# An MLP kernel's opening: the first transpose of x for one tile in place of two, and the loads behind it in another order

## The chip, the cores and the metric

The kernel runs on one core of a Trainium2 chip. The metric is the device time of one execution in microseconds, as the median of several runs. Times inside an execution come from a profile of one execution and count from its first instruction.

## The reference

The computation is a two-layer feed-forward block on 2048 tokens, in bf16. x has 640 features, the hidden layer 1728.

```
x: (1, 2048, 640)   w1: (640, 1728)   w2: (1728, 640)
h   = einsum("bsd,df->bsf", x, w1)
h   = silu(h)
out = einsum("bsf,fd->bsd", h, w2)
```

## The kernel before

TensorE contracts over the 128 partitions, so x must stand in SBUF with its features on partitions. `xT` holds x in this form: 5 tiles of 128 features (index k) by 2048 tokens. The form is made by DMA transposes straight from DRAM, all issued from the SP queue. The tokens are cut into 4 chunks of 512. w1 stands in `w1s` as 5 slabs, one for each k, of 1728 columns. The columns of h form 13 blocks of 128 (index ft) and a tail of 64.

The unit of work in the first stage is `step`: for one k, one block ft and one chunk, two matmuls of 64 columns of w1 each against 512 tokens, into the two halves of one PSUM bank. Five steps (k = 0 to 4) complete a block of one chunk; ScalarE then applies silu and writes `hT`.

The first chunk is treated apart, because its data have yet to arrive. Its first 8 blocks (1024 columns of w1) occupy the 8 PSUM banks at once, and the work goes k by k: for each k a sweep over the 8 blocks, so 8 steps need only tile k of x and the first 1024 columns of slab k. `opening` (line 197) first runs dummy matmuls on a zeroed tile `z` (line 132: 13 of 128 columns and one pair of 64 columns, each against 256 columns), then waits for the first transpose and the first 5 blocks of slab 0, does the sweep of k = 0, and calls `sweep` (line 192) for k = 1, 2, 3. Each sweep begins with a wait for its slab and its tile. The sweep for k = 4 follows, with the silus; then blocks 8 to 12 of chunk 0, five steps each, and then chunks 1 to 3, each behind a wait for its five transposes. TensorE works in program order, so a wait holds all that stands behind it.

The order of the transfers is written out by hand. `early` puts instructions ahead of the program's start-up barrier on an engine. The ACT queue issues the first 5 blocks of slab 0 (160 KB). The SP queue issues, in this order (lines 123 and 148 to 157): the transpose of tiles 0 and 1 for chunk 0; the other 3 blocks of slab 0 (96 KB); slab 1 (256 KB, 8 blocks); slab 2; the transpose of tile 2; slab 3; the transpose of tiles 3 and 4; slab 4; two loads with the remaining columns of all slabs (320 KB and 560 KB). Then come 15 transposes, one for each tile of chunks 1 to 3 (line 163), and the four loads of w2. Each transfer has a semaphore of its own; the five transposes of a chunk share one. `turned` (line 90) issues a transpose, `slab` (line 118) a part of a slab.

The second stage multiplies hT by w2, which has long arrived, evacuates the results through VectorE and ScalarE, and stores them. The change does not touch it.

Of the kernel before, what the change touches and what calls it, by code (L numbers as in the profile page):

```python
# [9 lines left out]
def bass_standalone__dense_activation_silu__prompt_kernel(  # L10
# [13 lines left out]
    P = 128  # L24
# [5 lines left out]
    SCH = 512  # L30
# [8 lines left out]
    pe, act, dve, pool, sp = nc.tensor, nc.scalar, nc.vector, nc.gpsimd, nc.sync  # L39

    with ExitStack() as es:
# [18 lines left out]
        def sem(name):  # L60
            s = es.enter_context(nc.semaphore(name))
            count[s.name if hasattr(s, "name") else name] = 0
            return [s, 0]

        def tick(ins, s, n=1):
            ins.then_inc(s[0], n)
            s[1] += n
            return (s, s[1])

        def wait(eng, *points):  # L70
            for pt in points:
                if pt is None:
                    continue
                s, v = pt
                key = (id(eng), id(s))
                if seen.get(key, 0) < v:
                    eng.wait_ge(s[0], v)
                    seen[key] = v
# [6 lines left out]
        def load(eng, out_ap, in_ap):  # L85
            s = sem(f"s_ld{n_dma[0]}")
            n_dma[0] += 1
            return tick(eng.dma_start(out=out_ap, in_=in_ap), s, 16)

        def turned(c0, c1, k0, k1):  # L90
            s = sem(f"s_tr{n_dma[0]}")
            n_dma[0] += 1
            return tick(sp.dma_start_transpose(
                out=xT[:, k0:k1, c0:c1], in_=xf[c0:c1, k0 * P:k1 * P]), s, 16)

        ET = mybir.EngineType

        def early(emit, engine, arrived=True):
            n = len(nc.main_func.blocks[0].instructions)
            r = emit()  # L100
            lst = nc.main_func.blocks[0].instructions
            new = lst[n:]
            del lst[n:]
            at = next(
                i for i, ins in enumerate(lst)
                if ins.opcode == ("EventSemaphore" if arrived else "Drain") and ins.engine == engine
            )
            lst[at:at] = new
            return r
# [4 lines left out]
        NO = NB  # L114
# [3 lines left out]
        def slab(eng, k, f0=0, f1=NO):  # L118
            return load(eng, w1s[:, k, f0 * P:f1 * P], w1_v[:, k, f0 * P:f1 * P])

        ld_w1 = {}
        ld_t = {}
        ld_t[0] = ld_t[1] = early(lambda: turned(0, SCH, 0, 2), ET.SP, False)
        ld_w1[0] = early(lambda: slab(act, 0, 0, NA), ET.Activation, False)
        p_z = early(lambda: tick(dve.memset(z[:, :], 0.0), s_dve), ET.DVE, False)  # L125

# [2 lines left out]
        def dummies(n, w):  # L129
            for _ in range(n):  # L130
                for c0 in range(0, P, w):
                    pe.matmul(ps[c0:c0 + w, 3, 0:HB], lhsT=z[:, 0:w], rhs=z[:, :],  # L132
                              start=True, stop=True)

        def first_dummies():
            wait(pe, p_z)
            dummies(13, P)
            dummies(1, HC)

        p_warm = early(lambda: tick(pool.memset(warm[:, :], 0.0), s_pool), ET.Pool, False)  # L140
# [5 lines left out]
        early(warm_up, ET.Activation, False)  # L146

        ld_w1b = early(lambda: slab(sp, 0, NA, NO), ET.SP, False)
        ld_w1[1] = early(lambda: slab(sp, 1), ET.SP, False)
        ld_w1[2] = early(lambda: slab(sp, 2), ET.SP, False)  # L150
        ld_t[2] = early(lambda: turned(0, SCH, 2, 3), ET.SP, False)
        ld_w1[3] = early(lambda: slab(sp, 3), ET.SP, False)
        ld_t[3] = ld_t[4] = early(lambda: turned(0, SCH, 3, DT), ET.SP, False)
        ld_w1[4] = early(lambda: slab(sp, 4), ET.SP, False)
# [28 lines left out]
        def step(b, k, ft, c0, c1, start=False, stop=False):  # L183
            for h0 in (0, HC):
                ins = mm(ps[h0:h0 + HC, b, :], w1s[:, k, ft * P + h0:ft * P + h0 + HC],
                         xT[:, k, c0:c1], start, stop, shared=True)
            return ins

        def part(k, ft, c0, c1, start=False, stop=False):
            return step(ft, k, ft, c0, c1, start, stop)  # L190

        def sweep(k, c0, c1, *waits):
            wait(pe, *waits)
            for ft in range(NO):
                part(k, ft, c0, c1)

        def opening():
            first_dummies()
            wait(pe, ld_t[0], ld_w1[0])
            for ft in range(NO):  # L200
                if ft == NA:
                    wait(pe, ld_w1b)
                part(0, ft, 0, SCH, start=True)
            for k in range(1, DT - 1):
                sweep(k, 0, SCH, ld_w1[k], ld_t[k])
# [206 lines left out]
```

## Time and profile before

| | us |
|---|---|
| median of 3 runs (lowest, highest) | 124.34 (124.25, 124.39) |
| the profiled execution | 124.57 |
| its span, first to last instruction | 123.1 |
| TensorE busy | 120.7 (98%) |
| ScalarE busy | 38.8 (32%) |
| VectorE busy | 6.9 (6%) |

The chain that ended last is TensorE for 98% of the span. Nothing but TensorE's own pace stands on it after its first instruction at 0.39 us, apart from pieces of 0.3 us and less. How the opening's transfers were issued from SP, and how long each took from its issue to its landing:

| transfer | issued at | issue took | landed after |
|---|---|---|---|
| transpose of tiles 0 and 1 | 0.00 | 1.33 | 3.4 |
| slab 0, last 3 blocks | 1.39 | 0.56 | 3.1 |
| slab 1 | 2.00 | 0.42 | 3.3 |
| slab 2 | 2.46 | 0.43 | 3.5 |
| transpose of tile 2 | 2.94 | 1.16 | 3.6 |
| slab 3 | 4.14 | 0.58 | 3.3 |
| transpose of tiles 3 and 4 | 4.76 | 1.24 | 3.7 |
| slab 4 | 6.04 | 0.59 | 4.1 |
| remaining columns, first load | 6.67 | 0.44 | 4.4 |
| remaining columns, second load | 7.15 | 0.53 | 5.6 |
| first transpose of chunk 1 | 8.07 | 1.46 | 5.2 |
| fifth transpose of chunk 1 | 13.48 | 2.21 | 4.4 |

The ACT queue's 160 KB of slab 0 were issued at 0.12 and landed after 2.4. A landing is issue time plus the last column. In the lines of the profile, PE stands for TensorE's matmuls, PEld for its weight loads, SPq and ACTq for the queues of SP and ScalarE, ACT for ScalarE, DVE for VectorE and POOL for GpSimd.

### The profile page before, as it was taken

The numbers are of one execution on the slowest core, as the hardware profiler recorded it, in microseconds if no ns is written. First come the engines' busy times: TensorE is split into PE (matmuls) and PEld (weight loads), VectorE is DVE, ScalarE is ACT, GpSimd is POOL, SyncE is SP. The second block draws the span as 40 slices with busy tenths as digits, with TensorE's granted clock in tenths as the row PEclk, the third lists the DMA queues.
The fourth block names the chain that finished last, engine by engine and source line by source line (L and its number), as shares of the span: only waits on it lengthen the run. The fifth ranks groups of instructions, "written<-read, shape, count | busy, mean of one in ns | idle before, by whom it ended". The sixth has DMA issues, their size and how long they took to land.

```text
span 123.1 us, 2300 instructions
## 1 busy us (share of the span) xinstructions
PE 120.7 (98%) x1056; PEld 59.5 (48%) x1057; DVE 6.9 (6%) x11; ACT 38.8 (32%) x67; POOL 0.3 (0%) x5
## 2 busy tenths in 40 slices
PE   8999999999999999999999999999999999999993
PEld 5455555555555555555544444444444444444452
DVE  0000000000000000000000022002201300222001
ACT  4002975555555555555530011001101200110110
POOL 0000000000000000000000000000000000000000
PEclk9999999999999999999999999999999999999999
DMA  6999935555992000000000004202200220023112
GB/s 146 263 248 315 135 86 108 104 87 92 280 392 77 0 0 0 8 0 0 0 0 5 0 12 113 51 0 107 107 0 5 107 107 0 5 107 117 53 67 83
DMA packets 19625, 10.42 MB, mean 85 GB/s; under 512 B 13728, under 2 KB 19104, under 8 KB 19616
## 3 DMA queue, kind: packets, MB, share of 16 engines
q1 hardware_dynamic: 19328, 10.08, 31.0%
q10 hardware_dynamic: 288, 0.20, 0.6%
q8 instruction: 8, 0.13, 0.5%
q14 instruction: 1, 0.01, 0.0%
HBM read 4.51 MB, written 2.62 MB: 58 GB/s over the span
## 4 chain that ended last, share of the span: by engine, by line
PE 98%; issue 0%; ACT 0%; DVEq 0%
PE ps L175 95%; PE ps L132 3%; ACT o_sb L256 0%; DVEq L397 0%
## 5 line engine op out<-in xcount | busy, mean ns | idle before, releaser
L175 PE MATMUL ps<-xT,w1s 128*64 128x512 bf16 x540 | 59.2, 382 | 0.0
L175 PE MATMUL ps<-w2s,hT 64*128 64x512 bf16 (+3 forms) x376 | 46.0, 369 | 0.2 <-issue 0.2
L175 PEld LDWEIGHTS ps<-xT,w1s 128*64 128x64 bf16 x540 | 30.6, 111 | 28.3 <-issue 0.9
L179 ACT ACTIVATE hT<-ps 128x512 bf16<-128x512 f32 x52 | 30.0, 608 | 29.2 <-PE ps L175 29.2
L175 PEld LDWEIGHTS ps<-w2s,hT 64*128 64x128 bf16 (+1 forms) x377 | 21.0, 95 | 24.1 <-issue 0.2
L256 ACT CAST o_sb<-ps 128x512 bf16<-128x512 f32 (+1 forms) x9 | 4.9, 550 | 41.5 <-PE ps L175 41.5
L175 PE MATMUL ps<-hT,w2s 64*128 64x512 bf16 x104 | 11.7, 376 | 0.0
L175 PEld LDWEIGHTS ps<-hT,w2s 64*128 64x128 bf16 x104 | 5.0, 94 | 6.3 <-issue 0.4
L254 DVE CAST o_sb<-ps 128x512 bf16<-128x512 f32 (+1 forms) x8 | 5.4, 675 | 40.5 <-PE ps L175 40.5
L254 DVE CAST oT<-ps 128x512 bf16<-128x512 f32 x2 | 1.4, 691 | 73.5 <-PE ps L175 73.5
L256 ACT CAST oT<-ps 128x512 bf16<-128x512 f32 x2 | 1.2, 585 | 10.6 <-PE ps L175 10.6
L132 PE MATMUL ps<-z 128*128 128x256 bf16 (+1 forms) x15 | 3.3, 419 | 0.4 <-DVE z L125 0.4
L175 PE MATMUL ps<-w2t,hTt 64*128 64x512 bf16 (+2 forms) x17 | 2.9, 363 | 0.0
L132 PEld LDWEIGHTS ps<-z 128*128 128x128 bf16 (+1 forms) x15 | 1.9, 143 | 1.5 <-issue 0.4
L179 ACT ACTIVATE hTt<-ps 128x512 bf16<-128x512 f32 x2 | 1.2, 597 | 1.0 <-PE ps L175 1.0
L144 ACT ACT_TABLE_LOAD x1 | 1.3, 1283 | 0.5 <-issue 0.5
L175 PEld LDWEIGHTS ps<-w2t,hTt 64*128 64x128 bf16 x17 | 0.9, 94 | 1.1
L175 PE MATMUL ps<-hTt,w2t 64*128 64x512 bf16 x4 | 0.8, 376 | 0.0
L175 PEld LDWEIGHTS ps<-hTt,w2t 64*128 64x128 bf16 x4 | 0.2, 94 | 0.2
L144 ACT ACTIVATE warm<-warm 128x32 f32<-128x32 f32 x1 | 0.2, 229 | 0.0
L125 DVE MEMSET z<- 128x128 uint32 x1 | 0.2, 165 | 0.2 <-issue 0.2
L140 POOL MEMSET warm<- 128x32 f32 x1 | 0.1, 124 | 0.0
(4 smaller groups left out, 0.4 us busy)
## 6 DMA issues: line engine op xcount, KB each, us to landing
out_dram<-o_sb SPq DMA_DIRECT2D x15, 160.0 KB, 1.8
w2s<-in_w_dram SPq DMA_DIRECT2D x1, 1120.0 KB, 6.6
w1s<-in_w_dram SPq DMA_DIRECT2D x4, 256.0 KB, 3.4
w2s<-in_w_dram SPq DMA_DIRECT2D x1, 960.0 KB, 8.6
w1s<-in_w_dram SPq DMA_DIRECT2D x1, 560.0 KB, 5.6
w1s<-in_w_dram SPq DMA_DIRECT2D x1, 320.0 KB, 4.4
xT<-in_x_dram SPq DMA_TRANSPOSE x18, 3.7
w1s<-in_w_dram ACTq DMA_DIRECT2D x1, 160.0 KB, 2.4
```

What stands on the lines that cost most here:

```text
L125: p_z = early(lambda: tick(dve.memset(z[:, :], 0.0), s_dve), ET.DVE, False)
L132: pe.matmul(ps[c0:c0 + w, 3, 0:HB], lhsT=z[:, 0:w], rhs=z[:, :], start=True, stop=True)
L140: p_warm = early(lambda: tick(pool.memset(warm[:, :], 0.0), s_pool), ET.Pool, False)
L144: act.activation(out=warm[:, :], in_=warm[:, :], func=ACT.Silu)
L175: return pe.matmul(o, lhsT=l, rhs=r, start=start, stop=stop, skip_group_check=shared)
L179: r = tick(act.activation(out=out_ap, in_=in_ap, func=ACT.Silu), s_act)
L254: r = tick(dve.tensor_copy(out=out_ap, in_=in_ap), s_dve)
L256: r = tick(act.copy(out=out_ap, in_=in_ap), s_act)
```

## The change

The first transpose brings tile 0 alone. Tiles 1 and 2 come in one transpose, which stands behind the rest of slab 0 and ahead of slab 1. Slab 1 comes as two loads of 4 blocks (128 KB each); `sweep` waits for the second of them ahead of block 4 of k = 1. Two dummies of 128 columns are taken out. Tiles 3 and 4, slabs 2 to 4 and all later transfers keep their order.

```
-        ld_t[0] = ld_t[1] = early(lambda: turned(0, SCH, 0, 2), ET.SP, False)
+        ld_t[0] = early(lambda: turned(0, SCH, 0, 1), ET.SP, False)
...
-            dummies(13, P)
+            dummies(11, P)
...
         ld_w1b = early(lambda: slab(sp, 0, NA, NO), ET.SP, False)
-        ld_w1[1] = early(lambda: slab(sp, 1), ET.SP, False)
+        ld_t[1] = ld_t[2] = early(lambda: turned(0, SCH, 1, 3), ET.SP, False)
+        ld_w1[1] = early(lambda: slab(sp, 1, 0, NO // 2), ET.SP, False)
+        ld_w1c = early(lambda: slab(sp, 1, NO // 2, NO), ET.SP, False)
         ld_w1[2] = early(lambda: slab(sp, 2), ET.SP, False)
-        ld_t[2] = early(lambda: turned(0, SCH, 2, 3), ET.SP, False)
         ld_w1[3] = early(lambda: slab(sp, 3), ET.SP, False)
...
             for ft in range(NO):
+                if k == 1 and ft == NO // 2:
+                    wait(pe, ld_w1c)
                 part(k, ft, c0, c1)
```

## The prediction

> **What bounds the kernel now.** I read the page first, then the chain of waits, then the opening 20 us of the timeline, then the same stretch cut into quarter microseconds with its DMA rates, and last the DMA issues one by one. The first two say that TensorE is the bound and has no hole:
>
> ```profile
> PE 120.7 (98%) x1056; PEld 59.5 (48%) x1057; DVE 6.9 (6%) x11; ACT 38.8 (32%) x67; POOL 0.3 (0%) x5
> ...
> 0.39 3.31 PE ps L132 x15
> 3.70 106.17 PE ps L175 x976
> ```
>
> The chain runs from the dummies of line 132 straight into the real matmuls. So every time that the change saves or costs in the opening goes one for one to the end, and any wait for a transfer that becomes late is new time. The timeline (start, length, engine, line) gives the rate of the opening:
>
> ```profile
> 3.28 0.13 PEld L132 LDWEIGHTS ps<-z 128*64 128x64 bf16 x2 [0.41 <-issue]
> 3.47 0.21 PEld L175 LDWEIGHTS ps<-xT,w1s 128*64 128x64 bf16 x4
> 3.49 18.86 PE L175 MATMUL ps<-xT,w1s 128*64 128x512 bf16 x166
> 3.92 0.18 PEld L175 LDWEIGHTS ps<-xT,w1s 128*64 128x64 bf16 x2 [0.25 <-issue]
> 4.35 0.18 PEld L175 LDWEIGHTS ps<-xT,w1s 128*64 128x64 bf16 x2 [0.25 <-issue]
> 4.78 0.18 PEld L175 LDWEIGHTS ps<-xT,w1s 128*64 128x64 bf16 x2 [0.25 <-issue]
> 5.13 16.95 PEld L175 LDWEIGHTS ps<-xT,w1s 128*64 128x64 bf16 x158 [0.18 <-issue]
> ```
>
> A step is a pair of half-width matmuls. Real work starts at 3.49. Steps start 0.43 apart up to 4.78, and from 5.13 on they are 0.216 apart (18.09 to 18.30 in a late stretch, in which sixty-one steps reach from 5.13 to 18.30). The profile prints the granted clock as 1.00 all along; the doubling of the pace at about 5.1, some 4.7 us after the first dummy, is what I go by. The SP queue, which issues almost all transfers, reads:
>
> ```profile
> 0.00 1.33 SPq L93 DMA_TRANSPOSE xT<-in_x_dram  x1
> 1.39 1.51 SPq L88 DMA_DIRECT2D w1s<-in_w_dram  x3
> 2.94 1.16 SPq L93 DMA_TRANSPOSE xT<-in_x_dram  x1
> 4.14 0.58 SPq L88 DMA_DIRECT2D w1s<-in_w_dram  x1
> 4.76 1.24 SPq L93 DMA_TRANSPOSE xT<-in_x_dram  x1
> 6.04 1.64 SPq L88 DMA_DIRECT2D w1s<-in_w_dram  x3
> 13.48 2.21 SPq L163 DMA_TRANSPOSE xT<-in_x_dram  x1
> ```
>
> A transpose holds SP for 1.16 (one tile) or 1.24 us (two), a load 0.42 to 0.59. From issue to landing, asked one by one (the last figure is us):
>
> ```profile
> xT<-in_x_dram SPq DMA_TRANSPOSE x1, 3.4
> w1s<-in_w_dram SPq DMA_DIRECT2D x1, 96.0 KB, 3.1
> w1s<-in_w_dram SPq DMA_DIRECT2D x1, 256.0 KB, 3.3
> ```
>
> These are the first transpose (lands 3.40), the rest of slab 0 (1.39 to 4.49) and slab 1 (2.00 to 5.30; the same 3.3 for slab 3, 4.14 to 7.44). Slab 2 took 3.5 (2.46 to 5.96), the transpose of tile 2 3.6 (2.94 to 6.54), that of tiles 3 and 4 3.7 (4.76 to 8.46), slab 4 4.1 (6.04 to 10.14). Sweep 1 starts at step 8, 5.13 + 4 x 0.216 = 5.99, so slab 1 was early by 0.7. Last, the DMA rate (last column, GB/s) around the first load that follows a transpose:
>
> ```profile
> 2.50:2.75 0.25, 0.25 (x3) 0.19 (x2) 0.00 (x0) 0.00 (x0) 0.00 (x0) 1.00 1.24 279
> 3.00:3.25 0.25, 0.25 (x2) 0.00 (x0) 0.00 (x0) 0.00 (x0) 0.00 (x0) 1.00 0.64 55
> 4.50:4.75 0.25, 0.25 (x4) 0.03 (x2) 0.00 (x0) 0.00 (x0) 0.00 (x0) 1.00 1.05 402
> ```
>
> Three loads are waiting at 3.0, and still the engines fall to 55 GB/s; they are back at 402 later. A load behind a transpose starts late, and this is what the change meets.
>
> **The change part by part.** *Two dummies fewer.* A dummy starts every 0.21 us (three in each quarter microsecond, counted with overlap; 13 between 0.39 and 3.28 are 0.22 each), so the dummies end about 0.43 earlier and the first step can start at 3.06. That is one slow step more before the pace doubles at 5.1, and each step done there takes one fast step from afterwards: the gain is 0.216 us, not 0.43. Steps would start at 3.06, 3.49, 3.92, 4.35, 4.78, 5.13, and sweep 1 would want to start at 5.13 + 3 x 0.216 = 5.78.
>
> *Tile 0 alone.* It must land by about 3.0. The two-tile transpose, alone on its queue, landed at 3.40, the quickest one-tile transpose of the trace took 2.9. By bytes: the first 416 KB (two tiles and the ACT queue's 160 KB) had passed at about 2.8, 288 KB (one tile and the same load) at about 2.35, so one tile is some 0.45 earlier, 2.95. Bounds 2.9 and 3.4; I take 2.95, no wait. At 3.4 the first step is 0.4 later, which costs 0.2 back at the slow pace.
>
> *SP's order.* Tile 0's issue: 1.33 less the 0.08 between two tiles and one, 1.25. Rest of slab 0: 1.31, 0.56 long. Tiles 1 and 2: 1.92, 1.24 long. First half of slab 1: 3.20, 0.58 long. Second half: 3.82, 0.43 long. Slab 2: 4.29; slab 3: 4.76; tiles 3 and 4: 5.24; slab 4: 6.52; then the two loads of the rest at 7.15 and 7.63. Against before, slab 1 is issued 1.2 us later, slab 2 1.8, slab 3 0.6, all behind 0.5; the transposes are two double and one single in both, so what is added is one load, 0.43 + 0.04.
>
> *The rest of slab 0* lands by 1.31 + 3.1 = 4.41; step 5 wants it at 5.13. *Tiles 1 and 2* land at 1.92 + 3.4 to 3.7 = 5.32 to 5.62, before 5.78: no wait, 0.2 to 0.4 in hand.
>
> *First half of slab 1*, the step that decides. It is the first load behind a two-tile transpose. Nearest row: the rest of slab 0 in the same place, 96 KB, 3.1, gives 6.30. The other rows behind a transpose are 3.3 (6.50) and 4.1 (7.30). A second way: that load landed 1.1 behind the transpose ahead of it, so 5.32 to 5.62 plus 1.1 = 6.4 to 6.7. The low end is the ACT queue's load of 160 KB, which has no transpose ahead: 2.4, landing 5.60, no wait at all. Its 32 KB more would cost some 0.1; that the ACT load no longer runs beside the transpose ahead gives as much back. I take 6.30, and 0.05 from there to the matmul (z's memset ends at 0.34, the first dummy starts at 0.39): sweep 1 starts at 6.35 in place of 5.99, 0.36 later than before, with TensorE idle for 0.57. PE is in order, so all else queues behind that wait.
>
> *Second half of slab 1.* Second load behind a transpose, like slab 1 (3.3): 3.82 + 3.3 = 7.12 at worst, since it is half of that size; wanted at 6.35 + 4 x 0.216 = 7.21. No wait. *Slab 2*: 4.29 + 3.5 = 7.79, wanted at 8.08. *Slab 3*: 8.06 to 8.9 against 9.80; *tiles 3 and 4*: 8.94 against 9.80; *slab 4*: 10.62 against 11.53; the rest 11.55 against 13.25. All covered, by 0.3 us and more, because the sweeps stand later; with no wait in sweep 1 slab 2 would have 0.28 less cover and wait 0.3.
>
> *Chunk 1's transposes* stand behind the added load. The last of the five was issued at 13.48 and took 4.4, landing 17.88, and chunk 1 starts at 18.30. Shifted by 0.47 it lands at 18.35; if the backlog sets it (its issue took 2.21 against 1.26) at 17.88. With 0.36 of delay chunk 1 wants it at 18.66: hidden. Without that delay it would be the next wait: at most 18.40 against 18.30, 0.10 slower than before in place of 0.216 faster. Later chunks have over 5 us.
>
> Sum: -0.216 + 0.57 = +0.36 us (rounded). Against the profiled execution, 124.57 (span 123.1 and 1.47 around it), that is 124.93; that execution stands 0.23 over the median of the runs, 124.34, so the forecast is **124.70**, slower by 0.29%. About 0.2%, 0.25 us, is what a measurement of this kernel can tell from no change.
>
> **The rivals.** *A, not slower: the load behind the transpose comes without the gap.* If the first half lands by 6.18 the result is within the bound, and it decides at 5.73, where no wait is left. For it: it is half a slab, slab 3 followed the one-tile transpose of tile 2 by 0.9 us for 256 KB, so half of it may come 0.5 behind, near 5.9 to 6.1; and the rate after that transpose hardly dipped. Against it: the dip to 55 GB/s, and 109 GB/s at 7.75 behind the transpose of tiles 3 and 4. Its time: between 124.34 - 0.22 = 124.12 (nothing waits) and 124.59, likeliest 124.44 where chunk 1's transposes cap it. The Trainium skill (Advanced Engine Details and Errata, X-Bar Transpose) says that transpose DMAs on TRN2 are as fast as regular ones; by that rule the half slab would follow at the loads' pace, 5.32 + 0.33 = 5.65 by the 402 GB/s row, and this rival would hold. The trace of before does not agree in this place, by the 1.1 us of the first load. Chance 0.23.
>
> *B, much slower: the load comes as late as slab 4 did, or a hole before 5.1 delays the faster pace.* A landing at 7.30 gives 7.35 - 5.99 = +1.36, 125.70. If tile 0 lands at 3.4, TensorE is idle for 0.35 inside the stretch that precedes the doubling; were that to put the doubling off by 2 us, it costs another 1.0. For it: the first transpose did land only at 3.40. Against: slab 4 had far more queued ahead, and tile 0 has half the bytes. Chance 0.08: 125.1 to 125.8. The Trainium skill (TensorE: Matmul & The Clock Gate, on the clock gate) has the clock released after a busy window of some 3.4 us, and the window free-running, so that the place of the doubling would move from run to run; three runs within 0.14 us of each other do not show such a spread.
>
> *C, faster beyond the bound.* In runs without the profiler the first transpose may land after the dummies end, so that TensorE waits today and tile 0 alone saves 0.5 us or more of it, and A holds as well: 123.95 to 124.09. The trace has the two within 0.1 us (3.40 and 3.49), so it is open; but a saving there counts half, for the pace. Chance 0.07.
>
> **How the numbers follow.** Forecast, 124.59 to 125.1 (the second way's end, 6.71, gives +0.77): 0.62. A 0.23, B 0.08, C 0.07. Slower: 0.62 + 0.08, and 0.02 of A, whose upper edge lies on the bound, 0.72; same 0.20; faster 0.08 (C and A's lowest edge). The range leaves out B, C and the lowest of A: 124.20 to 125.10; the forecast's own is 124.59 to 125.1.
>
> **What would show it.** In the trace after: 13 dummies instead of 15; real work from 3.06, five slow steps; the first half of slab 1 issued at about 3.2 and landing at about 6.3; TensorE idle once, for 0.4 to 0.8 us, ahead of sweep 1 near 5.8; no idle at the sweep's middle, at sweep 2 or at chunk 1. Wrong would be: no hole at 5.8 (A), a hole before 5.1 (B), a hole ahead of chunk 1 near 18.3 (the added load).

## The result and the profile after

The changed kernel took 125.31 us (median of 18 runs, 124.99 to 126.33) against 124.50 for the kernel before on the same chip (18 runs, 123.91 to 125.37): a ratio of 1.0061, 95% interval 1.0044 to 1.0078, slower. Ratios here and below leave out executions of more than 1.5% above the fastest of their kernel, so a ratio can differ from that of two medians. The profiled execution took 125.07 (span 123.6), 0.50 more than the one before.

The chain of waits of the changed kernel no longer starts with TensorE, but with SP:

```profile
by line: PE ps L176 93.4%; DMA w1s<-in_w_dram 2.5%; SPq L93 2.0%; SPq L88 0.5%; ACT o_sb L259 0.2%; issue 0.2%
...
1.92 1.25 SPq L93
3.17 0.04 issue
3.22 3.09 DMA w1s<-in_w_dram
6.30 0.04 issue
6.35 115.39 PE ps L176 x1025
```

It runs through SP's issue of the transpose of tiles 1 and 2 (1.92), the first half of slab 1 (3.22 to 6.3) and into sweep 1. The timeline of the opening (start, length, engine, line, and in brackets the idle time before) has the holes:

```profile
3.10 0.18 PEld L176 LDWEIGHTS ps<-xT,w1s 128*64 128x64 bf16 x4
4.38 0.18 PEld L176 LDWEIGHTS ps<-xT,w1s 128*64 128x64 bf16 x2 [0.25 <-issue]
4.81 0.62 PEld L176 LDWEIGHTS ps<-xT,w1s 128*64 128x64 bf16 x6 [0.25 <-issue]
6.34 0.57 PEld L176 LDWEIGHTS ps<-xT,w1s 128*64 128x64 bf16 x8 [0.91 <-DMA w1s<-in_w_dram]
6.35 15.85 PE L176 MATMUL ps<-xT,w1s 128*64 128x512 bf16 x144 [0.43 <-DMA w1s<-in_w_dram]
7.32 4.03 PEld L176 LDWEIGHTS ps<-xT,w1s 128*64 128x64 bf16 x40 [0.40 <-DMA w1s<-in_w_dram]
11.64 10.29 PEld L176 LDWEIGHTS ps<-xT,w1s 128*64 128x64 bf16 x98 [0.30 <-DMA w1s<-in_w_dram]
19.00 0.60 ACT L180 ACTIVATE hT<-ps 128x512 bf16<-128x512 f32 x1 [0.48 <-PE ps L176]
```

Real work starts at 3.10, 0.39 earlier. Sweep 1 waits until 6.35 for the first half of slab 1; the sweep's middle waits until 7.32, some 0.1 beyond 6.35 + 4 x 0.216; slab 4 comes just as it is wanted (11.64), so that only a weight load waits for it and no matmul. The bracket of 0.43 counts from the modelled end of the matmul before; a fast step would have started at 5.75, so sweep 1 is 0.60 late. A mark for the whole opening is the start of chunk 1. It stands 0.21 ahead of the silu of chunk 0's last block: 18.30 against 18.51 in the trace before, and 18.79 against 19.00 here. The line of the trace before:

```profile
18.51 0.60 ACT L179 ACTIVATE hT<-ps 128x512 bf16<-128x512 f32 x1 [0.48 <-PE ps L175]
```

The 0.49 that chunk 1 is later is the whole difference of the two spans (0.5); nothing is lost or won behind it.

The moment at which TensorE's pace doubles is read from the step that spans it, the one whose length is between 0.427 and 0.216: 5.06 in the trace before, 4.96 here. It is called the moment below. The first step after a wait takes 0.24 at the fast pace too (5.17 to 5.41 in the second trace of the kernel before), so a first step of 0.24 only says that the moment lies at its start or before.

### The profile page after: what moved, and what is told of

Same layout as the page of the kernel before. It is cut to its first block, busy times and chain, and to the rows that moved or that the text cites. A ratio compares the mean times of both kernels' runs of the same rounds, so it can differ in the third digit from the quotient of the medians.

```text
span 123.6 us, 2298 instructions
## 1 busy us (share of the span) xinstructions
PE 120.9 (98%) x1055; PEld 59.5 (48%) x1055; DVE 6.9 (6%) x11; ACT 38.8 (31%) x67; POOL 0.3 (0%) x5
## 4 chain that ended last, share of the span: by engine, by line
PE 93%; DMA 2%; SPq 2%; ACT 0%; issue 0%
PE ps L176 93%; DMA w1s<-in_w_dram 2%; SPq L93 2%; SPq L88 0%; ACT o_sb L259 0%
```

## The experiments

Each is a kernel of its own. Its time stands beside runs of the kernel before on the same chip, with the ratio to it.

**The changed kernel again, three more traces, and the kernel before, two more.** The code is as above.

> The changed kernel again, for a second trace of it and a second comparison. Theory (late transfers): TensorE idles ahead of sweep 1 until the first half of slab 1 lands at about 6.3, and has no cover left at the second half and at slab 4, so that in many executions there are further waits of 0.1 to 0.4 us there; 0.7 to 0.9 us slower than the kernel before. Rival (pace): the doubling of TensorE's pace comes at another time than in the kernel before; then the steps stay 0.43 us apart past 5.5 in this trace, and the waits alone sum to 0.5.

> The changed kernel, one more trace. Theory (arrivals set the opening unless the pace doubles late): chunk 1 starts at 18.7 to 19.3 in any case; with a doubling before 5.7 there is a hole ahead of sweep 1 and the first half of slab 1 lands at 5.9 to 6.4; with one after 6.2 there is none. Rival (the wait is a constant of the kernel): a hole of 0.4 to 0.6 whatever the moment, and the start of chunk 1 moves with half of the moment.

> The changed kernel, a third trace of it beside the first two. Theory: chunk 1 starts at 18.7 to 19.3 whatever the moment of the doubling, with a hole ahead of sweep 1 if that is before 5.7. Rival: a hole of 0.4 to 0.6 in any case, and the start of chunk 1 moves with half of the moment.

> The kernel before, one more trace. Theory: with a doubling at 4 to 7 chunk 1 starts at 17.51 + (moment - 3.49)/2, 17.8 to 19.2, without waits of over 0.1, and at the earliest moments the arrivals hold it at about 18.1. Rival: the start of chunk 1 does not follow the moment.

> The kernel before again, for a second trace. If the doubling of the pace comes at a place that is drawn anew in each execution, this trace has it elsewhere than at 5.06, its time moves by half of the difference, and no wait for a transfer of slab 1 to 4 appears; if the place belongs to the kernel, it is at 5.06 again within 0.2.

The second comparison gave 125.02 (12 runs) against 124.51, ratio 1.0032 (1.0007 to 1.0058). It overlaps with the first one between 1.0044 and 1.0058, so a loss of about 0.5% satisfies both.

Of the second trace of the changed kernel, the opening's slow steps and the last silu of chunk 0:

```profile
4.78 0.18 PEld L176 LDWEIGHTS ps<-xT,w1s 128*64 128x64 bf16 x2 [0.25 <-issue]
6.06 0.18 PEld L176 LDWEIGHTS ps<-xT,w1s 128*64 128x64 bf16 x2 [0.25 <-DMA w1s<-in_w_dram]
6.48 13.53 PEld L176 LDWEIGHTS ps<-xT,w1s 128*64 128x64 bf16 x126 [0.25 <-issue]
19.03 0.60 ACT L180 ACTIVATE hT<-ps 128x512 bf16<-128x512 f32 x1 [0.48 <-PE ps L176]
```

There is no hole: the steps are 0.43 apart until the moment at about 6.6, and such a slow TensorE wants slab 1 only when it is there (5.9 in this trace). Slow steps past 5.5 are the sign that the first expectation gave for its rival, pace; yet the time is that of the first trace. The third trace has the moment at about 4.9 and a hole:

```profile
6.47 14.87 PE L176 MATMUL ps<-xT,w1s 128*64 128x512 bf16 x136 [0.57 <-DMA w1s<-in_w_dram]
19.00 0.60 ACT L180 ACTIVATE hT<-ps 128x512 bf16<-128x512 f32 x1 [0.48 <-PE ps L176]
```

The kernel before, in its second trace:

```profile
3.68 0.79 PEld L175 LDWEIGHTS ps<-xT,w1s 128*64 128x64 bf16 x10 [0.27 <-DMA xT<-in_x_dram]
5.17 15.52 PE L175 MATMUL ps<-xT,w1s 128*64 128x512 bf16 x142 [0.22 <-DMA w1s<-in_w_dram]
18.36 0.60 ACT L179 ACTIVATE hT<-ps 128x512 bf16<-128x512 f32 x1 [0.48 <-PE ps L175]
```

The first five steps already run at the fast pace (ten matmuls in 1.27), so the moment lies at 3.7 or before, and now this kernel waits too: 0.22 for the rest of slab 0, which took 3.7 to land in place of 3.1. All traces side by side (chunk 1's start is the last silu's less 0.21):

| trace | moment | hole ahead of sweep 1 | chunk 1 starts | time |
|---|---|---|---|---|
| before, first | 5.06 | none | 18.30 | 124.57 |
| before, second | 3.7 or before | none (0.22 in sweep 0) | 18.15 | 124.45 |
| before, third | about 3.9 | none (0.30 in sweep 0) | 18.30 | 124.61 |
| changed, first | 4.96 | 0.43 | 18.79 | 125.07 |
| changed, second | 6.6 | none | 18.82 | 125.08 |
| changed, third | 4.9 | 0.57 | 18.79 | 125.05 |
| changed, fourth | 6.2 | none | 18.72 | 124.98 |

The rival of a constant wait falls: the hole is there or not, and chunk 1 starts at 18.72 to 18.82 all the same. The theory's second half needs mending: the kernel before does not follow the moment below 5 either, because its own transfers then hold it at 18.15 to 18.30. In these traces the changed kernel's level is 0.53 higher (means 18.78 and 18.25), and the mean times are 0.50 apart (125.05 and 124.54).

These means don't compare like with like, since two of the changed kernel's moments are later than any of the kernel before. By the formula of the expectation above, 17.51 + (moment - 3.49)/2, the kernel before would start chunk 1 at 18.87 and 19.07 with moments of 6.2 and 6.6, behind the changed kernel's 18.72 and 18.82. That is an estimate; no trace of the kernel before has so late a moment. At moments of 4.9 to 5.1, where both have traces, the changed kernel is 0.49 behind (18.79 against 18.30). Four moments against three can't tell whether the changed kernel doubles its pace later as a rule; the next run tests one possible cause of that, the fewer dummies.

**The two dummies put back.** The earlier start is undone, the rest of the change stays.

```
-            dummies(11, P)
+            dummies(13, P)
```

> The changed kernel with the two dummies put back (13). Theory (late transfers): sweep 0 starts 0.43 later but sweep 1 still starts when the first half of slab 1 has landed, at about 6.35, so the time is that of the changed kernel within 0.15 us: 0.8 slower than the kernel before. If the earlier start was a gain that is kept: 0.2 slower than the changed kernel. Rival (pace): if fewer dummies put the doubling off, this kernel gets back 0.3 us or more of the 0.8.

It took 125.16 (12 runs) against 124.51, ratio 1.0050 (1.0028 to 1.0073). That lies between the two results of the changed kernel, so neither a kept gain nor a loss by fewer dummies is to be seen. In its trace the earlier start would have been worth nothing, because sweep 1 begins when slab 1 is there. The moment is very early (3.8), and there is a further wait, ahead of chunk 1:

```profile
6.03 12.77 PE L176 MATMUL ps<-xT,w1s 128*64 128x512 bf16 x114 [0.49 <-DMA w1s<-in_w_dram]
18.84 0.60 ACT L180 ACTIVATE hT<-ps 128x512 bf16<-128x512 f32 x1 [0.48 <-PE ps L176]
19.30 1.05 PE L176 MATMUL ps<-xT,w1s 128*64 128x512 bf16 x8 [0.50 <-DMA xT<-in_x_dram]
```

Chunk 1 could have started at 18.63 and starts at 19.30: its fifth transpose was issued at 14.82 and took 4.4, landing at 19.25. The prediction held this one to be hidden, with an issue 0.47 later than the 13.48 of the kernel before. In the four traces of the changed kernel it was issued at 14.1 to 14.7, took 3.2 to 3.5 and landed at 17.3 to 18.2, and no matmul waited for it. So the added load is not the whole of this wait, nor is the early moment: a landing at 19.25 is late for a start at 18.8 too.

**Two dummies fewer in the kernel before**, nothing else.

```
-            dummies(13, P)
+            dummies(11, P)
```

> The kernel before with two dummies fewer, all else as it was. Tile 0 and 1 land at 3.4, so TensorE idles from 3.06 to about 3.44 and starts 0.05 earlier than before. Theory (late transfers): within 0.15 us of the kernel before. Rival (pace: a hole ahead of the doubling puts it off by a whole window of some 3.4 us, as the 0.93 us hole did, where the doubling came at 8.0): 0.3 us or more slower on the median, with a wider spread.

It took 124.68 against 124.67, ratio 1.0028 (0.9999 to 1.0057). The first transpose landed at 3.7 in the trace, TensorE stood still for 0.49 before it, and the moment came at about 5.1, within the range of the other traces. Five of the twelve runs lie at 125.3 to 126.0, where the kernel before has none over 125.25 on this chip. So nothing is won on the median, and whether a part of the runs had the doubling put off is not shown by this one trace.

**Slab 1 whole.**

```
-        ld_w1[1] = early(lambda: slab(sp, 1, 0, NO // 2), ET.SP, False)
-        ld_w1c = early(lambda: slab(sp, 1, NO // 2, NO), ET.SP, False)
+        ld_w1[1] = early(lambda: slab(sp, 1), ET.SP, False)
...
-                if k == 1 and ft == NO // 2:
-                    wait(pe, ld_w1c)
```

> The changed kernel with slab 1 as one load again, in the place of its first half. SP issues one load less, so slab 2 and all later transfers are issued 0.47 us earlier. Theory (late transfers): slab 1 is issued at 3.2 and lands 3.3 to 3.6 later, 6.5 to 6.8, so sweep 1 starts 0.2 to 0.5 later than with the halves, but there is no second wait, and slab 4 and chunk 1's transposes have more cover; between 0.1 faster and 0.3 slower than the changed kernel, 0.7 to 1.1 slower than before. Rival (the added load costs the time, by shifting all that stands behind it): 0.3 us or more faster than the changed kernel.

It took 125.74 against 124.51, ratio 1.0078 (1.0051 to 1.0106), slower than the changed kernel rather than faster, by 0.7 between the medians on this chip (125.02), which is also more than the theory's 0.3. The load took 4.1, not 3.3 to 3.6. It was issued at 3.23, with slabs 2 and 3 right behind it at 3.85 and 4.32; that they share the engines with it is the likely reason. This is its hole:

```profile
7.40 12.93 PE L175 MATMUL ps<-xT,w1s 128*64 128x512 bf16 x118 [1.68 <-DMA w1s<-in_w_dram]
```

The halves are worth their extra issue in this place: they let sweep 1 begin 1 us earlier (6.35 against 7.40).

**The halves alone, in the kernel before.** Transposes and order are as before.

```
-        ld_w1[1] = early(lambda: slab(sp, 1), ET.SP, False)
+        ld_w1[1] = early(lambda: slab(sp, 1, 0, NO // 2), ET.SP, False)
+        ld_w1c = early(lambda: slab(sp, 1, NO // 2, NO), ET.SP, False)
...
+                if k == 1 and ft == NO // 2:
+                    wait(pe, ld_w1c)
```

> The kernel before with slab 1 alone in two halves, the wait for the second at the middle of sweep 1. The added load, alone: slab 2, the transpose of tile 2 and all later transfers are issued 0.47 us later, in the old order. Theory (late transfers, mostly by the two-tile transpose ahead of slab 1): cover of 0.5 us and more takes it, 0.0 to 0.25 slower than before. Rival (the added load makes the loss): 0.4 or more slower than before.

It took 124.95 (12 runs) against 124.43, ratio 1.0031 (1.0005 to 1.0056), 0.4 us. That stands at the edge of the rival, but the interval reaches from 0.06 to 0.70 us and excludes neither side; it does exclude that the added load is free. In the trace the moment is at about 4.5, and TensorE waits for tiles 3 and 4, issued at 5.23 in place of 4.76 and landing 4.5 later in place of 3.7 to 4.2 in the three traces of the kernel before:

```profile
9.85 11.41 PE L176 MATMUL ps<-xT,w1s 128*64 128x512 bf16 x104 [0.49 <-DMA xT<-in_x_dram]
```

**Slab 1 ahead of tiles 1 and 2.**

```
-        ld_t[1] = ld_t[2] = early(lambda: turned(0, SCH, 1, 3), ET.SP, False)
         ld_w1[1] = early(lambda: slab(sp, 1, 0, NO // 2), ET.SP, False)
         ld_w1c = early(lambda: slab(sp, 1, NO // 2, NO), ET.SP, False)
+        ld_t[1] = ld_t[2] = early(lambda: turned(0, SCH, 1, 3), ET.SP, False)
```

> The changed kernel with both halves of slab 1 ahead of the transpose of tiles 1 and 2. Theory (late transfers): slab 1 lands at 4.6 to 5.4, and the wait moves to the transpose: issued at 2.9, landing 3.2 to 3.6 later, 6.1 to 6.5, against 5.78; the hole ahead of sweep 1 is of the same size or 0.2 smaller, and slab 2 and the later ones stay as late as in the changed kernel: 0.3 to 0.9 us slower than before. If the place behind the transpose were what makes slab 1 late, and the transpose itself were not held up: 0.0 to 0.2 slower than before.

It took 125.44 (6 runs) against 124.67, ratio 1.0067 (1.0049 to 1.0085). As expected the wait moves from the slab to the transpose:

```profile
6.66 14.14 PE L176 MATMUL ps<-xT,w1s 128*64 128x512 bf16 x128 [1.34 <-DMA xT<-in_x_dram]
```

Tiles 1 and 2, issued at 2.91, landed at 6.5; slab 1's halves had landed at 4.5 and 5.4. Sweep 1 needs both, SP issues them one behind the other, and the second of the two comes at 5.9 to 6.5 in either order. In the kernel before, tile 1 came with tile 0, and slab 1 was the only thing that sweep 1 waited for.

**The same cover for both: 44 dummies.** Real work starts near 7, so that the transfers are ahead of it.

```
-            dummies(13, P)
+            dummies(44, P)
```

In the changed kernel the same line has 11 in place of 13.

> The kernel before with 44 dummies in place of 13, so that real work starts at 6.6 to 8.3, whatever the moment of the doubling, and every transfer has more cover. Both theories: no wait for a transfer in the opening; 2 to 3 us slower than the kernel before. It is the base for the next run.

> The changed kernel with 44 dummies in place of 11, to be held against the kernel before with 44. Theory (late transfers): with real work from 6.6 to 8.3, sweep 1 wants slab 1 at 8.3 or later, and it lands at 6.0 to 6.4; slab 4, wanted at 13.5, lands at 10.5 to 11.6; so no wait is left and the two differ by less than 0.2 us. Rival (the new order costs something besides those waits: slower transfers all along, the added load, the later second stage): 0.5 to 0.8 us slower than the kernel before with 44.

The kernel before took 127.63 with it, ratio 1.0259 (1.0227 to 1.0291); the changed one 128.05, ratio 1.0285 (1.0246 to 1.0324). The intervals overlap, so by time it is undecided; the start of real work is drawn with the moment. The traces tell more. Their last but one silu of chunk 0, and the start of real work:

```profile
7.03 14.20 PE L175 MATMUL ps<-xT,w1s 128*64 128x512 bf16 x130
20.19 0.60 ACT L179 ACTIVATE hT<-ps 128x512 bf16<-128x512 f32 x1 [0.33 <-PE ps L175]
```

The changed kernel:

```profile
6.80 14.41 PE L176 MATMUL ps<-xT,w1s 128*64 128x512 bf16 x132
19.96 0.60 ACT L180 ACTIVATE hT<-ps 128x512 bf16<-128x512 f32 x1 [0.33 <-PE ps L176]
```

From the first to the second line both need 13.16, and neither has a hole. The times of these two executions, 127.32 and 127.08, differ by 0.24, as their starts do (0.23). With cover, the new order costs nothing in these two traces, as it should if the waits are the loss. The medians, 0.42 apart, lie between what the two sides allowed and do not confirm it.

**Four attempts to take a load from SP.** Slab 1 whole on the ACT queue; the same, held back until the warm-up activation has ended; the rest of slab 0 on the ACT queue; and that one held back.

```
         early(warm_up, ET.Activation, False)
+        ld_w1[1] = early(lambda: slab(act, 1), ET.Activation, False)
...
-        ld_w1[1] = early(lambda: slab(sp, 1, 0, NO // 2), ET.SP, False)
-        ld_w1c = early(lambda: slab(sp, 1, NO // 2, NO), ET.SP, False)
...
-                if k == 1 and ft == NO // 2:
-                    wait(pe, ld_w1c)
```

> The changed kernel with slab 1 as one load from the ACT queue, issued behind the warm-up activation at about 2.1, so that it doesn't stand behind the transpose of tiles 1 and 2, and SP issues one load less than in the kernel before. Theory (late transfers): slab 1 lands at about 5.0 to 5.4, before sweep 1 wants it at 5.78; sweep 1 starts at 5.78 or when tiles 1 and 2 land, 5.4 to 5.6; the whole 0.8 goes and the 0.2 of the earlier start is kept: 124.3, 0.0 to 0.25 faster than the kernel before. Rival (pace, or the earlier start itself): stays 0.3 us or more slower than the kernel before with no hole ahead of sweep 1.

```
-            act.activation(out=warm[:, :], in_=warm[:, :], func=ACT.Silu)
+            wait(act, tick(act.activation(out=warm[:, :], in_=warm[:, :], func=ACT.Silu), s_act))
```

> The changed kernel with slab 1 as one load from the ACT queue, held there until the warm-up activation has ended, about 2.1 (in the run before it, the load left at 0.60, took the engines from tile 0, which landed at 4.2, and TensorE stood still for 0.93). SP issues one load less than the kernel before. Theory (late transfers): slab 1 lands at 5.0 to 5.5, tile 0 near 3.1, tiles 1 and 2 at 5.2 to 5.7; no hole ahead of sweep 1 where the pace doubles at 5 or later; at most 0.1 slower and at best 0.25 faster than the kernel before, about 1 us faster than the changed kernel with slab 1 whole on SP. Rival (pace): with no hole the time still is 0.3 or more over the kernel before.

```
         ld_w1[0] = early(lambda: slab(act, 0, 0, NA), ET.Activation, False)
+        ld_w1b = early(lambda: slab(act, 0, NA, NO), ET.Activation, False)
...
-        ld_w1b = early(lambda: slab(sp, 0, NA, NO), ET.SP, False)
```

> The changed kernel with the rest of slab 0 moved from SP to the ACT queue, right behind its first part. SP then issues tiles 1 and 2 at 1.3 in place of 1.9 and the halves of slab 1 at 2.6 and 3.2 in place of 3.2 and 3.8, and as many transfers as the kernel before. Theory (late transfers): the first half lands at 5.4 to 5.7, 0.6 earlier than in the changed kernel, and nearly all of the loss goes: 0.1 faster to 0.3 slower than the kernel before, if tile 0 still lands by 3.3. What can undo it: 96 KB more beside the transpose of tile 0; if that makes tile 0 land at 3.6 or later, TensorE stands still ahead of the doubling, and it is 0.3 or more slower.

For the last one, that load stands behind the held warm-up of the second.

> The changed kernel with the rest of slab 0 on the ACT queue, held there until the warm-up activation has ended, about 2.1, so that it stands beside tiles 1 and 2 and not beside tile 0. SP issues tiles 1 and 2 at 1.3 and the halves of slab 1 at 2.6 and 3.2, and as many transfers as the kernel before. Theory (SP's row makes slab 1 late): tile 0 lands at 3.1, tiles 1 and 2 at 4.6 to 5.2, the first half at 5.4 to 5.8, 0.5 earlier than in the changed kernel; 0.1 faster to 0.3 slower than the kernel before, and at least 0.3 faster than the changed one. Rival (the transposes suffer under any load beside them): tiles 1 and 2 land at 5.5 or later, and it is no faster than the changed kernel.

| kernel | median | ratio (interval) | tile 0 landed | tiles 1, 2 landed | longest hole | moment |
|---|---|---|---|---|---|---|
| slab 1 on ACT | 126.51 | 1.0084 (1.0037 to 1.0130) | 4.2 | 5.4 | 0.93, ahead of tile 0 | 8.0 |
| the same, held | 126.05 | 1.0064 (1.0036 to 1.0092) | 3.1 | 9.1 | 3.19, ahead of sweep 1 | about 5.2 |
| rest of slab 0 on ACT | 126.29 | 1.0067 (1.0024 to 1.0110) | 4.1 | 4.9 | 0.85, ahead of tile 0 | 8.4 |
| the same, held | 126.43 | 1.0126 (1.0080 to 1.0172) | 3.8 | 5.8 | 0.59, ahead of tile 0 | 3.9 or before |

All four missed. By the medians, which leave no execution out, they are 2.00, 1.38, 1.86 and 1.71 slower than the kernel before on the same chip. In none of the traces was the case reached that the kernel was made for, since a transpose came late each time. The traced executions took 126.40, 129.21, 126.51 and 125.09; the second is one of three at 129 among eleven, and does not stand for the other eight, at 125.0 to 126.8. In the last one the first half of slab 1 was issued at 2.61, 0.6 earlier than in the changed kernel, and landed at 6.1, only 0.2 earlier. So that SP's row of issues alone makes slab 1 late is not shown: in this trace an earlier issue brought only a third of itself at the landing. It has what its rival named, tiles 1 and 2 landing after 5.5 and no gain on the changed kernel. The third one shows what a hole ahead of the doubling can do:

```profile
4.13 17.15 PE L176 MATMUL ps<-xT,w1s 128*64 128x512 bf16 x138 [0.85 <-DMA xT<-in_x_dram]
7.98 0.18 PEld L176 LDWEIGHTS ps<-xT,w1s 128*64 128x64 bf16 x2 [0.25 <-issue]
8.39 12.63 PEld L176 LDWEIGHTS ps<-xT,w1s 128*64 128x64 bf16 x118 [0.23 <-issue]
```

The steps stay 0.43 apart until about 8.4. Its twelve runs fall into three of 124.5 to 124.7 and nine of 126.0 to 127.2; the first one of the four has the same split (two of 124.7 and 124.8, ten of 126.1 to 128.1). In none of the traces without a hole over 0.6 ahead of real work does the doubling come after 6.6. That the hole put it off is the likeliest reading, on two traces.

## Why the prediction was right and wrong

The direction, the place and the mechanism were right where the pace doubles near 5, as the forecast took it to; two of the four traces have the hole, and two have slow steps in its place. The size was too small, and the time lies outside the range. Of the 0.61 between 124.70 and 125.31, 0.16 is the kernel before, whose median is 124.50 and not 124.34, 0.13 is found in the trace after, and some 0.3 stays open.

- **Earlier start.** Forecast 3.06, measured 3.10; tile 0 took 3.1, forecast 2.95, which is the 0.04. Right.
- **The half slab.** Forecast: issued 3.20, landing 6.30, matmuls from 6.35. Measured 3.22, 6.32, 6.35. The row of the 96 KB load in the same place was the right one; that it hit to 0.02 is partly luck, since the other three traces have the landing at 5.9 to 6.4. TensorE's delay was forecast as 0.57 and was 0.60. Rival A falls: the half landed 0.9 behind tiles 1 and 2 (5.42), not 0.5. In two further traces (the changed kernel's second and the one with 13 dummies) it landed by 6.0, inside A's condition of 6.18, and they took 125.08 and 125.57, so the condition alone does not bring A's time. The Trainium skill's rule that transposes are as fast as regular DMAs (Advanced Engine Details and Errata, X-Bar Transpose) does not give this gap; the trace has it.
- **The covers behind it.** This step failed: "All covered, by 0.3 us and more". The second half, whose cover was 0.09 by the forecast's own sum (7.12 against 7.21), took 3.4, not 3.3 for twice the size, and held TensorE until 7.32, 0.1 late. Slab 4 was forecast to land at 10.62 against 11.53; it was issued at 6.88 and not at 6.52, because the issue of tiles 3 and 4 took 1.57 in place of 1.24, took 4.7 in place of 4.1, and landed at 11.58 against 11.64: a cover of 0.9 was used up, though no matmul waited. The landing times came from one execution; the two later traces of the kernel before have slab 1 at 3.8 and 3.9 in place of 3.3. Covers of 0.1 to 0.9 are not covers against that spread.
- **The sum.** Forecast +0.36 against a profiled execution. The first traces of both, with nearly the same moment, are 0.50 apart in time and 0.49 at chunk 1. The missing 0.13 at chunk 1 is 0.11 for the second half and 0.02 for the first step of sweep 1, which takes 0.24 after the wait.
- **The median.** The first comparison's 0.81 is 0.3 more than the traces, and the cause of that stays open; the second comparison's medians are 0.51 apart, as the traces are. Two traces of neighbouring kernels, with moments of 3.8 and 4.5, show waits that the forecast called hidden: 0.50 ahead of chunk 1 in the run with 13 dummies, 0.49 for tiles 3 and 4 in the run with the halves alone. The halves alone cost 0.4 (0.06 to 0.70), which the forecast had at nothing. No trace of the changed kernel has these waits; whether its executions without a trace do is not measured, and the two comparisons of the same kernel (1.0061 and 1.0032) differ by as much as is to be explained.
- **Rival B's clock.** The forecast read the moment from one trace, put it at 5.1 for both kernels, and took three runs within 0.14 us for a sign that it is steady. In further traces it lies at 3.2 (the changed kernel with 44 dummies) to 6.6. The Trainium skill (TensorE: Matmul & The Clock Gate, on the clock gate) says that the window is free-running and the number of slow matmuls varies from run to run; the traces agree, and spread wider than its 0.5 us either way. The measured 125.31 falls into B's 125.1 to 125.8 without B's mechanism having been seen: in the changed kernel's traces no hole stands ahead of the doubling, and the half slab landed at 5.9 to 6.4, not at 7.30.
- **Rival C** falls: the fastest of 30 runs of the changed kernel is 124.61, and the kernel before reaches 123.91. Its premise holds in part: in the second and third trace of the kernel before the first transpose landed at 3.6 and TensorE waited for it, starting at 3.68 and 3.67 in place of 3.49. What that saves is lost again ahead of sweep 1.

## What to carry to other kernels

In an opening that is fed by one queue, making the first transfer smaller only helps if what the next part of the work needs isn't pushed back by more; here the start came 0.39 earlier and sweep 1 began 0.35 later. Work out a change's covers from several executions: a cover smaller than the spread of the landings is a wait in some of them. Where the pace of the consumer changes at a moment drawn anew, do the sum at an early and at a late moment, since an early one shows the waits and a late one hides them.

## What the runs showed of the hardware

- The pace of TensorE doubled between 3.2 and 6.6 us in traces of nearly the same code, 2.8 to 6.2 after its first matmul. The earliest is that of the changed kernel with 44 dummies, whose dummies start 0.21 apart up to 3.13 and 0.11 apart from 3.30 on. Two traces with a hole of 0.85 and 0.93 ahead of it had it at 8.4 and 8.0; one with 0.59 and one with 0.49 had it by 3.9 and at 5.1.
- After a hole of 3.19 us in the second of the four attempts, steps that had been 0.216 apart were 0.43 apart again from 9.67 to 11.8, and the profile's granted clock reads 0.50 from 8.7 to 12.0 and 1.00 before and after.
- Transposes landed later in traces with more beside or right behind them; which neighbour did it is not separated. Tile 0 landed after 2.9 to 3.1 with 160 KB beside it (four traces of the changed kernel), after 4.2 with 256 KB more from the ACT queue, and after 3.8 with the next transpose issued right behind it and no further load until 2.1. Tiles 1 and 2 took 3.1 to 3.5, and 3.5 too with slab 1 issued from the ACT queue at 0.60; with slab 1 issued there at 2.10 they took 7.2, in the one traced execution of 129.21. The Trainium skill (DMA: Bandwidth & Descriptors, Rules for kernel authors) says that spreading transfers over issuing engines doesn't help bandwidth, since they share the same 16 DMA engines; the four attempts, slower by 1.38 to 2.00 between medians, do not speak against it.
- Of loads from the same place behind tiles 1 and 2, 128 KB took 2.7 to 3.2 (four traces) and 256 KB 4.1 (one), with more loads right behind both.
